# Block-diagonal global values, PSUM banks by token block and turned gate products in a local/global attention with top-k routing

## The chip, the cores and the metric

The kernel runs on one core of one Trainium2 chip. The metric is the device time of one execution in microseconds (us); lower is better. Each kernel is timed in several runs and the median is given. A separate execution is recorded by the hardware profiler, and all durations below come from that one.

## The reference

The first half is attention over 8 batches, 8 heads, 512 local and 32 global tokens of 64 elements. Global queries see all 544 keys; a local query sees the 32 global keys and the local keys at a distance of at most 32:

```
s_g  = scale * q_g @ k_all^T                      # k_all = [k_g, k_l]
out_g = softmax(s_g) @ v_all
s_l  = [scale * q_l @ k_g^T,  where(|i-j| <= 32, scale * q_l @ k_l^T, -1e9)]
out_l = softmax(s_l) @ v_all                      # x = concat(out_g, out_l): 4352 rows of 512
```

The second half sends each row of x to one of 8 experts and keeps the 80 rows with the largest gate of each expert:

```
logits = x @ w_gate;  expert = argmax;  gate = softmax(logits)[expert]
out[kept rows of e] = gate * (relu(x @ w1[e]) @ w2[e]);  all other rows are 0
```

## The kernel before, in words

A **quarter** q (16 of them) is half of a batch: four heads, two pairs j = 0, 1. A quarter passes through these chunks:

- `load_qk`, `load_v`: DMAs, one to two quarters ahead. `vb` holds the values of 32 global and 512 local tokens in five blocks, with a column of ones after each 64 (the softmax sum falls out of the product). `spread_v` on POOL makes a copy shifted by 64 partitions for the odd blocks.
- `T_chunk`: eight fp16 transposes on PE of the queries and keys of a pair, then two copies on ACT (L227) from PSUM into `qkT`. Rows were loaded with i = 4 neighbouring tokens in a partition, so the copy also reorders: it reads PSUM in order and writes every fourth element.
- `S_chunk`: scores. `G_ps` (global keys by all local queries), `gq_ps` (global queries), and `l_ps`, one bank per head: 8 blocks of 64 queries by a window of 128 keys. Even blocks are one product of 128 weight columns (L258); odd blocks are two of 64, each half written to the partitions that put its keys in the order of the shifted values (L266). ACT takes the exponential of each; DVE (first head of a pair) or POOL (second head) multiplies by the band mask (L273).
- `G_chunk`: values of the global keys, 16 products with 32 rows each (a head's 32 global keys lie in partitions 32h to 32h+31) into four PSUM tiles `o_ps`, one for each head (L289).
- `H_chunk(q, h)`: for head h, eight products `eL` by `vb`, which add to the head's bank (L302); then DVE's reciprocal of the sums and the scaling into `xn`.
- `Q_chunk`: the global queries' output. `X_chunk`: `xn` transposed (fp32, L333), copied by DVE to `xT`.
- `L_chunk(b)`: gate logits, 16 products for the local tokens with 128x128 of `xT` as weights and the 8 gate columns moving (L351), four for the global ones (L354); then softmax, argmax and first tie on DVE. `K_chunk` after batches 3, 6 and 7 runs rounds of max and replace on DVE (L412, L414) to find the 80 largest per expert.

After attention: the last selection rounds, the loading of the five experts that did not fit before (their memory is that of the attention), gather, two layers per expert, scatter. Weights of three experts are loaded during batches 0 to 2.

The order of chunks is that of the main loop, but a scheduler interleaves the instructions of neighbouring chunks on each engine; each engine then runs its own list in order. Pools give the buffers: two PSUM banks for `T` (T_ps, x_ps, lg), two for `S` (scores), four for `O` (o_ps, og). An fp32 product appears in the trace as two instructions, each with its weight load.

Of the kernel before, what the change touches and what calls it, by code (L numbers as in the profile page):

```python
# [18 lines left out]
P = 128  # L19
# [7 lines left out]
def _np_consts(B, S, SG, cap):  # L27
    c = {}
    c["ident16"] = np.eye(P, dtype=np.float16)
    c["identf"] = np.eye(P, dtype=np.float32)  # L30
    p = np.arange(P)[:, None]
    i = np.arange(64)[None, :]
    band = np.zeros((P, 8, 64), dtype=np.float32)
    for t in range(8):
        w = p if t % 2 == 0 else (p + 64) % P
        key = 64 * t + w
        band[:, t, :] = (w - i >= 0) & (w - i <= 2 * WIN) & (key >= SG) & (key < S)
    c["band"] = band
# [12 lines left out]
    rm5 = np.ones((P, NB, 8), dtype=np.float32)  # L51
    rm5[:, :, 0] = 0.0
    c["rmask5"] = rm5
    return c


@with_exitstack
def kernel(
# [37 lines left out]
    def psT(shape, dt, name):  # L96
        return ps.tile(shape, dt, tag="T", bufs=2, name=name)
# [4 lines left out]
    def psO(shape, dt, name):  # L102
        return ps.tile(shape, dt, tag="O", bufs=4, name=name)
# [45 lines left out]
    def load_v(b):  # L149
        v = vb[b % 2]  # L150
        nc.sync.dma_start(out=v[0:32, 0, :, 0:64], in_=v_g[b].rearrange("h g d -> g h d"))
        nc.sync.dma_start(out=v[32:128, 0, :, 0:64], in_=v_l[b, :, 0:96].rearrange("h g d -> g h d"))
        for u in range(1, 4):
            nc.sync.dma_start(out=v[:, u, :, 0:64],
                              in_=v_l[b, :, 128 * u - 32:128 * u + 96].rearrange("h p d -> p h d"))
        nc.sync.dma_start(out=v[0:32, 4, :, 0:64], in_=v_l[b, :, 480:512].rearrange("h g d -> g h d"))

    def spread_v(b):
        v = vb[b % 2]
        nc.gpsimd.tensor_copy(out=v[0:64, 5:9], in_=v[0:64, 1:5])  # L160
        nc.gpsimd.tensor_copy(out=v[64:128, 5:9], in_=v[64:128, 0:4])

    load_v(0)

    vgb = apool.tile([P, B, 2, 65], FP32, name="vgb")
    nc.vector.memset(vgb[:, :, :, 64:65], 1.0)
    nc.sync.dma_start(out=vgb[:, :, :, 0:64].rearrange("p b q d -> p (b q) d"),
                      in_=v_g.rearrange("b (q f) g d -> (f g) (b q) d", f=4))
    wg = cpool.tile([P, 4, E], FP32, name="wg")
    nc.sync.dma_start(out=wg, in_=moe_w_gate.rearrange("(c p) e -> p c e", p=P))  # L170

    wgq = cpool.tile([P, 4, E], FP32, name="wgq")
    for q in range(2):
# [38 lines left out]
    def T_chunk(q, j):  # L212
        b, qd = divmod(q, 2)
        pr = 2 * qd + j
        buf = qkT[(2 * q + j) % 4]
        for f in range(2):
            nc.gpsimd.tensor_copy(out=buf[64 * f:64 * f + 64, 512:544],  # L217
                                  in_=kbd[64 * f:64 * f + 64, b, pr, 32 * f:32 * f + 32])
        T_ps = psT([P, 2, 512], FP16, f"T_ps{q}_{j}")
        for t in range(2):  # L220
            for i in range(4):
                nc.tensor.transpose(out=T_ps[:, t, 128 * i:128 * i + 128],  # L222
                                    in_=qkr[q][:, t, i, 2 * j:2 * j + 2, :],
                                    identity=ident16[:, :])
        dst = buf[:, 0:1088].rearrange("x (t y) -> x t y", t=2)[:, :, 0:512]
        for t, eng in ((0, nc.scalar.copy), (1, nc.scalar.copy)):
            eng(out=dst[:, t].rearrange("x (p i) -> x i p", i=4),  # L227
                in_=T_ps[:, t].rearrange("x (i p) -> x i p", i=4))

    def S_chunk(q, j):  # L230
        b, qd = divmod(q, 2)
# [20 lines left out]
        s["eQ"].append(eQ)  # L252

        l_ps = [psS([P, 512], FP32, f"l_ps{q}_{j}_{hh}") for hh in range(2)]
        for t in range(0, 8, 2):
            for hh in range(2):
                o = 64 * hh
                nc.tensor.matmul(out=l_ps[hh][:, 64 * t:64 * t + 64],  # L258
                                 lhsT=buf[o:o + 64, 512 + 64 * t:640 + 64 * t],
                                 rhs=buf[o:o + 64, 64 * t:64 * t + 64], start=True, stop=True)  # L260
        for t in range(1, 8, 2):
            for half in range(2):
                for hh in range(2):
                    o = 64 * hh
                    k0 = 512 + 64 * (t + 1 - half)
                    nc.tensor.matmul(out=l_ps[hh][64 * half:64 * half + 64, 64 * t:64 * t + 64],  # L266
                                     lhsT=buf[o:o + 64, k0:k0 + 64],
                                     rhs=buf[o:o + 64, 64 * t:64 * t + 64], start=True, stop=True)
# [7 lines left out]
    def G_chunk(q):  # L276
        b, qd = divmod(q, 2)
        s = st[q]
        bs = bst.setdefault(b, {})
        if qd == 0:  # L280
            bs["xg"] = lpool.tile([P, 2, 64], FP32, tag="xgn", name=f"xgn{b}")
            bs["xb"] = lpool.tile([P, 4, XW], FP32, tag="xb", name=f"xb{b}")
            bs["xT"] = []
        s["o"] = [psO([P, 4, 65], FP32, f"o_ps{q}_{h}") for h in range(4)]
        s["xn"] = hpool.tile([P, 4, 256], FP32, tag="xn", name=f"xn{q}")
        for u in range(4):
            for h in range(4):
                r = slice(32 * h, 32 * h + 32)
                nc.tensor.matmul(out=s["o"][h][:, u, :], lhsT=s["eG"][r, 128 * u:128 * u + 128],  # L289
                                 rhs=vgb[r, b, qd, :], start=(u == 0), stop=False,  # L290
                                 skip_group_check=True)

    def H_chunk(q, h):
        b, qd = divmod(q, 2)
        s = st[q]
        v = vb[b % 2]
        hd = 4 * qd + h
        o = s["o"][h]
        for u in range(4):
            for odd in range(2):  # L300
                t = 2 * u + odd
                nc.tensor.matmul(out=o[64 * odd:64 * odd + 64, u, :], lhsT=s["eL"][h][:, 64 * t:64 * t + 64],  # L302
                                 rhs=v[:, 5 * odd + u, hd, :], start=False, stop=(u == 3),
                                 skip_group_check=True)
        rec = hpool.tile([P, 4], FP32, tag="rec", bufs=4)
        nc.vector.reciprocal(out=rec[:], in_=o[:, :, 64])  # L306
        nc.vector.tensor_tensor(out=s["xn"][:, :, 64 * h:64 * h + 64], in0=o[:, :, 0:64],  # L307
                                in1=rec[:].unsqueeze(2).to_broadcast([P, 4, 64]), op=ALU.mult)

    def Q_chunk(q):  # L310
# [16 lines left out]
    def X_chunk(q, j):  # L327
        b, qd = divmod(q, 2)
        s = st[q]
        bs = bst[b]  # L330
        x_ps = psT([P, 512], FP32, f"x_ps{q}_{j}")
        for u in range(4):
            nc.tensor.transpose(out=x_ps[:, 128 * u:128 * u + 128],  # L333
                                in_=s["xn"][:, u, 128 * j:128 * j + 128], identity=identf[:, :])
        xT = hpool.tile([P, 512], FP32, tag="xT", bufs=5, name=f"xT{q}_{j}")
        nc.vector.tensor_copy(out=xT[:], in_=x_ps[:])  # L336
        bs["xT"].append(xT)
        if j == 1:
            nc.gpsimd.tensor_copy(out=bs["xb"][:, :, 128 * qd:128 * qd + 128].bitcast(BF16), in_=s["xn"][:])

    def L_chunk(b):
# [118 lines left out]
    for q in range(NQ):  # L460
# [28 lines left out]
                K_chunk(g)  # L489
            pending = None  # L490
        H_chunk(q, 2)
        X_chunk(q, 0)
        if nxt:
            S_chunk(q + 1, 1)
        H_chunk(q, 3)
        Q_chunk(q)
        X_chunk(q, 1)
        st.pop(q)
        if qd == 1:
# [148 lines left out]
```

## Time and profile before

| | us |
|---|---|
| median of 3 runs (lowest to highest) | 457.93 (449.67 to 462.68) |
| the profiled execution's own time | 452.65 |
| its span, first to last instruction | 450.9 |
| PE busy | 332.3 (74%) |
| DVE, POOL, ACT busy | 212.5, 173.8, 142.5 |

The span has a long first part with attention, in which PE is busy nearly all of the time (from 18 to 340 us), and a second part of about 110 us with little work on PE until the last 38 us. [...] The record of the clock begins at 47 us; what the views show as 1.0 before that is not a record.

### The profile page before, as it was taken

How to read it: one execution, taken by the hardware profiler on the slowest of the kernel's cores; microseconds unless marked ns; L12 is line 12 of the kernel's file. 1: busy time of each engine (PE TensorE's matmuls, PEld its weight loads, DVE VectorE, ACT ScalarE, POOL GpSimd, SP SyncE). 2: the span in 40 equal slices, each digit the busy share in tenths (PEclk: the TensorE clock that was granted, in tenths of full speed). 3: DMA queues.
4: the chain of work that ended last, by engine and by line, in shares of the span. 5: the costliest groups of instructions: out<-in, count | busy, mean ns of one | idle time of the engine just before them, and what ended most of it. 6: DMA issues, size and time to landing. Idle time of an engine off the chain costs nothing. (4 is left out here: it accounts for less than half of the span.)

```text
span 450.9 us, 10118 instructions
## 1 busy us (share of the span) xinstructions
PE 332.3 (74%) x4268; PEld 271.3 (60%) x4268; DVE 212.5 (47%) x558; ACT 142.5 (32%) x201; POOL 173.8 (39%) x248
## 2 busy tenths in 40 slices
PE   0289899989999998989998999889961001203984
PEld 0268678878777887868886878778861000202662
DVE  4262633452733544298257633534755998200221
ACT  1193362374266256243524233563000000000221
POOL 6273660763755534255341532132140143311131
PEclk9999956598579569578658555895565555555999
DMA  9999799799999468215005400101011099998111
GB/s 151 174 197 341 121 173 190 254 138 192 185 201 173 91 197 135 34 51 100 6 12 94 92 4 1 48 6 34 17 27 49 4 199 208 210 210 161 31 45 44
DMA packets 84525, 51.87 MB, mean 115 GB/s; under 512 B 48472, under 2 KB 77568, under 8 KB 84480
## 3 DMA queue, kind: packets, MB, share of 16 engines
q0 software_dynamic: 34896, 27.75, 39.8%
q1 hardware_dynamic: 49584, 23.48, 20.6%
q8 instruction: 33, 0.54, 0.5%
q14 instruction: 12, 0.10, 0.1%
HBM read 62.25 MB, written 14.70 MB: 171 GB/s over the span
## 5 line engine op out<-in xcount | busy, mean ns | idle before, releaser
L227 ACT COPY qkT<-T_ps 128x512 f16<-128x512 f16 x64 | 77.7, 1369 | 94.0 <-PE T_ps L222 94.0
L273 POOL TENSOR_TENSOR eL<-eL,band 128x512 f32<-128x512 f32 x32 | 42.3, 1321 | 80.6 <-ACT eL L271 70.2
L302 PE MATMUL o_ps<-vb,eL 128*64 128x65 f32 x1024 | 70.2, 281 | 0.1
L302 PEld LDWEIGHTS o_ps<-vb,eL 128*64 128x64 f32 x1024 | 55.3, 184 | 9.4 <-issue 3.1
L271 ACT ACTIVATE eL<-l_ps 128x512 f32<-128x512 f32 x64 | 37.0, 600 | 60.6 <-PE l_ps L266 59.0
L289 PE MATMUL o_ps<-vgb,eG 32*128 32x65 f32 x512 | 52.6, 363 | 0.9 <-DVE xgn L324 0.7
L351 PE MATMUL lg<-wg,xT 128*128 128x8 f32 x256 | 46.2, 318 | 5.8 <-ACT qkT L227 5.3
L289 PEld LDWEIGHTS o_ps<-vgb,eG 32*128 32x128 f32 x512 | 45.8, 263 | 7.5 <-issue 4.8
L351 PEld LDWEIGHTS lg<-wg,xT 128*128 128x128 f32 x256 | 44.7, 271 | 7.5 <-ACT qkT L227 6.0
L273 DVE TENSOR_TENSOR eL<-eL,band 128x512 f32<-128x512 f32 x32 | 26.1, 819 | 28.6 <-ACT eL L271 28.6
L217 POOL COPY qkT<-kbd 64x32 f16<-64x32 f16 x64 | 16.1, 251 | 55.4 <-PE l_ps L258 43.3
L602 ACT ACTIVATE hT<-h_ps 128x320 bf16<-128x320 f32 x16 | 7.0, 437 | 94.8 <-PE h_ps L600 94.2
L306 DVE RECIPROCAL rec<-o_ps 128x4 f32<-128x4 f32 x64 | 10.6, 171 | 43.4 <-PE o_ps L302 42.9
L333 PE MATMUL x_ps<-identf,xn 128*128 128x128 f32 x128 | 28.6, 366 | 2.9 <-DVE xn L307 2.2
L222 PE MATMUL T_ps<-ident,qkr 128*128 128x128 f16 x256 | 26.5, 261 | 1.4 <-DVE kbd L198 0.9
L130 DVE COPY qkr<-qk 128x1024 f16<-128x1024 f16 x32 | 21.3, 686 | 12.9 <-DMA qk<-in_q_l_dram 6.7
L336 DVE COPY xT<-x_ps 128x512 f32<-128x512 f32 x32 | 21.8, 680 | 11.1 <-PE x_ps L333 10.8
L307 DVE TENSOR_TENSOR xn<-o_ps,rec 128x256 f32<-128x256 f32 x64 | 26.3, 416 | 1.2
L258 PE MATMUL l_ps<-qkT 64*128 64x64 f16 x256 | 22.6, 221 | 3.9 <-ACT eQ L251 3.7
L317 PE MATMUL og<-vb,eQ 128*32 128x65 f32 x640 | 25.3, 279 | 0.0
L358 DVE COPY L<-lg 128x32 f32<-128x32 f32 x8 | 1.5, 191 | 50.4 <-PE lg L354 50.4
L535 PE MATMUL thr_ps<-dthr,ones 8*128 8x8 f32 x2 | 0.6, 351 | 33.6 <-DVE dthr L533 33.6
(109 smaller groups left out, 501.1 us busy)
## 6 DMA issues: line engine op xcount, KB each, us to landing
out_dram<-zt SPq DMA_DIRECT2D x17, 512.0 KB, 6.2
w1sb<-in_moe_w_dram POOLq DMA_DIRECT2D x8, 1024.0 KB, 13.6
w2sb<-in_moe_w_dram POOLq DMA_DIRECT2D x8, 1024.0 KB, 17.4
vb<-in_v_l_dram SPq DMA_DIRECT2D x24, 256.0 KB, 6.4
x_scr<-xb SPq DMA_DIRECT2D x8, 514.0 KB, 3.3
qk<-in_q_l_dram POOLq DMA_DIRECT2D x16, 256.0 KB, 4.8
qk<-in_k_l_dram POOLq DMA_DIRECT2D x16, 256.0 KB, 5.1
vb<-in_v_l_dram SPq DMA_DIRECT2D x8, 192.0 KB, 7.2
```

What stands on the lines that cost most here:

```text
L222: nc.tensor.transpose(out=T_ps[:, t, 128 * i:128 * i + 128], in_=qkr[q][:, t, i, 2 * j:2 * j + 2, :], identity=ident16[:, :])
L227: eng(out=dst[:, t].rearrange("x (p i) -> x i p", i=4), in_=T_ps[:, t].rearrange("x (i p) -> x i p", i=4))
L258: nc.tensor.matmul(out=l_ps[hh][:, 64 * t:64 * t + 64], lhsT=buf[o:o + 64, 512 + 64 * t:640 + 64 * t], rhs=buf[o:o + 64, 64 * t:64 * t + 6 ...
L271: nc.scalar.activation(out=eL[:], in_=l_ps[hh][:], func=AF.Exp, scale=scale)
L273: eng.tensor_tensor(out=eL[:], in0=eL[:], in1=band[:].rearrange("p t i -> p (t i)"), op=ALU.mult)
L289: nc.tensor.matmul(out=s["o"][h][:, u, :], lhsT=s["eG"][r, 128 * u:128 * u + 128], rhs=vgb[r, b, qd, :], start=(u == 0), stop=False, skip_ ...
L302: nc.tensor.matmul(out=o[64 * odd:64 * odd + 64, u, :], lhsT=s["eL"][h][:, 64 * t:64 * t + 64], rhs=v[:, 5 * odd + u, hd, :], start=False, ...
L307: nc.vector.tensor_tensor(out=s["xn"][:, :, 64 * h:64 * h + 64], in0=o[:, :, 0:64], in1=rec[:].unsqueeze(2).to_broadcast([P, 4, 64]), op=A ...
L317: nc.tensor.matmul(out=og[32 * h:32 * h + 32, :], lhsT=s["eQ"][h // 2][:, u, 32 * (h % 2):32 * (h % 2) + 32], rhs=v[:, u, 4 * qd + h, :], ...
L333: nc.tensor.transpose(out=x_ps[:, 128 * u:128 * u + 128], in_=s["xn"][:, u, 128 * j:128 * j + 128], identity=identf[:, :])
L336: nc.vector.tensor_copy(out=xT[:], in_=x_ps[:])
L351: nc.tensor.matmul(out=lg[:, u, :], lhsT=bs["xT"][cc][:, 128 * u:128 * u + 128], rhs=wg[:, cc, :], start=(cc == 0), stop=(cc == 3))
```

## The change

- `vbd` (two buffers, loaded per batch by four DMAs) holds the global values of a quarter block-diagonally: rows 32f to 32f+31 carry head f's values in columns 65f to 65f+64 and zeros elsewhere. One product with 128 rows and 260 columns replaces four with 32 rows and 65 columns each, per block u of 128 queries.
- `H_chunk(q, u)` now does one block of 128 tokens for all four heads, into one bank per block; `G_chunk` has no products of its own.
- The odd key windows are written by DVE into `kO` with their 64-key halves swapped, so that an odd block is also one product of 128 weight columns.
- The two copies of `T_chunk` stay on ACT, but write in order and read PSUM in steps of 128 elements; keys come first.
- `X_chunk`'s copy moves from DVE to ACT; both X chunks come after `Q_chunk`; `xT` has 4 buffers for 5.
- Gate logits: four products with the gate weights (8 columns padded to 32) as weights and 512 tokens of `xT` moving, each into its own 32 partitions of one bank; ACT copies the bank; four products with a selection matrix `sel` sum the four parts and turn them.

```diff
+    sel = np.zeros((P, 8), dtype=np.float32)          # sel[32*cc : 32*cc+8] = eye(8)
...
+        for f in range(4):
+            nc.sync.dma_start(out=vbd[b % 2][32 * f:32 * f + 32, :, f, 0:64],
+                              in_=v_g[b].rearrange("(q f) g d -> f g q d", f=4)[f])
...
-        for t, eng in ((0, nc.scalar.copy), (1, nc.scalar.copy)):
-            eng(out=dst[:, t].rearrange("x (p i) -> x i p", i=4),
-                in_=T_ps[:, t].rearrange("x (i p) -> x i p", i=4))
+        nc.scalar.copy(out=dst[:, 1].rearrange("x (p i) -> x p i", i=4),
+                       in_=T_ps[:, 1].rearrange("x (i p) -> x p i", i=4))
+        halves = buf[:, 512:1152].rearrange("x (u y) -> x u y", y=64)
+        for w in range(2):
+            nc.vector.tensor_copy(out=kO[(2 * q + j) % 4][:, :, w, :], in_=halves[:, 2 - w:10 - w:2, :])
+        nc.scalar.copy(out=dst[:, 0]...)               # the queries, in the same way
...
+        for t in range(8):                             # S_chunk
             for hh in range(2):
+                lhsT = buf[o:o + 64, 512 + 64 * t:640 + 64 * t]   # even t; odd t: kO[o:o + 64, t // 2]
+                nc.tensor.matmul(out=l_ps[hh][:, 64 * t:64 * t + 64], lhsT=lhsT,
                                  rhs=buf[o:o + 64, 64 * t:64 * t + 64], start=True, stop=True)
...
-                nc.tensor.matmul(out=s["o"][h][:, u, :], lhsT=s["eG"][r, 128 * u:128 * u + 128],
-                                 rhs=vgb[r, b, qd, :], start=(u == 0), stop=False,
+    def H_chunk(q, u):
+        o = psO([P, 4, 65], FP32, f"o_ps{q}_{u}")
+        nc.tensor.matmul(out=o[:].rearrange("p h d -> p (h d)"), lhsT=s["eG"][:, 128 * u:128 * u + 128],
+                         rhs=vbd[b % 2][:, qd].rearrange("p h d -> p (h d)"), start=True, stop=False,
+        for h in range(4):
             for odd in range(2):
                 t = 2 * u + odd
+                nc.tensor.matmul(out=o[64 * odd:64 * odd + 64, h, :],
+                                 lhsT=s["eL"][h][:, 64 * t:64 * t + 64],
+                                 rhs=v[:, 5 * odd + u, 4 * qd + h, :], start=False, stop=True,
...
-        nc.vector.tensor_copy(out=xT[:], in_=x_ps[:])
+        nc.scalar.copy(out=xT[:], in_=x_ps[:])
...
+        for cc in range(4):                            # L_chunk
+            nc.tensor.matmul(out=lt_ps[32 * cc:32 * cc + 32, :], lhsT=wg[:, cc, :], rhs=bs["xT"][cc][:],
+        nc.scalar.copy(out=lt[:], in_=lt_ps[:])
         for u in range(4):
-            for cc in range(4):
-                nc.tensor.matmul(out=lg[:, u, :], lhsT=bs["xT"][cc][:, 128 * u:128 * u + 128],
-                                 rhs=wg[:, cc, :], start=(cc == 0), stop=(cc == 3))
+            nc.tensor.matmul(out=lg[:, u, :], lhsT=lt[:, 128 * u:128 * u + 128], rhs=sel[:],
```

Three places show how the lists move. On PE, at the seam of two quarters in batch 2 (og is `Q_chunk`'s output, the last number of a name is a buffer), before, from the global values to the second head:

```order
L289 MATMUL o_ps_3_1288<-vgb,eG_1113 128x65
L302 MATMUL o_ps_0_1285<-vb_88,eL_0_0_1149 64x65 x8
L222 MATMUL T_ps_1_1319<-ident_76,qkr_1267 128x128
L302 MATMUL o_ps_1_1286<-vb_88,eL_0_1_1152 64x65 x8
L241 MATMUL G_ps_1341<-qkT_120,kbd 64x512
```

and at a seam of the changed kernel, from the last scores of a quarter to its first block of values:

```order
L279 MATMUL l_ps_1_1_2032<-qkT_135,kO_139 128x64
L309 MATMUL o_ps_3_2055<-vb_89,eL_1_1_1850 64x65
L325 MATMUL og_2068<-vb_89,eQ_0_1726 32x65 x2
L341 MATMUL x_ps_0_2092<-identf,xn_1929 128x128 x4
L341 MATMUL x_ps_1_2099<-identf,xn_1929 128x128 x4
L303 MATMUL o_ps_0_2141<-vbd_96,eG_1974 128x260
L233 MATMUL T_ps_0_2125<-ident_76,qkr_2120 128x128
L309 MATMUL o_ps_0_2141<-vb_88,eL_0_0_2002 64x65 x2
L309 MATMUL o_ps_0_2141<-vb_88,eL_1_1_2052 64x65 x2
```

(Rows of the same chunk between these are left out.) The first block of values needed `eL` of one head before, and needs that of all four heads now, eL_1_1 of the scores just above among them.

The gate logits of a batch on PE, before:

```order
L344 MATMUL xgT_ps_1384<-identf,xgn_764 128x128
L302 MATMUL o_ps_2_1287<-vb_88,eL_1_0_1209 64x65
L351 MATMUL lg_1388<-wg,xT_0_941 128x8
L351 MATMUL lg_1388<-wg,xT_1_1025 128x8
L351 MATMUL lg_1388<-wg,xT_0_1171 128x8
L351 MATMUL lg_1388<-wg,xT_1_1255 128x8
```

(these four come three times in a row, then the scores of one head, then once more) and now:

```order
L358 MATMUL lt_ps_2221<-xT_0_1895,wg 32x512
L279 MATMUL l_ps_0_0_2193<-qkT_136 128x64
L358 MATMUL lt_ps_2221<-xT_1_1902,wg 32x512
L358 MATMUL lt_ps_2221<-xT_0_2097,wg 32x512
L358 MATMUL lt_ps_2221<-xT_1_2104,wg 32x512
L303 MATMUL o_ps_2_2316<-vbd_96,eG_1974 128x260
L364 MATMUL lg_2228<-sel,lt 128x8 x4
L367 MATMUL lg_2228<-wgq,xgT 32x8 x4
```

One wide product stands ahead of a head's scores, three follow together, and the sums come some 20 products later.

ACT's list around the seam, before:

```order
L271 ACTIVATE eL_1_0_2574<-l_ps_1_0_2548 128x512
L271 ACTIVATE eL_1_1_2577<-l_ps_1_1_2549 128x512
L227 COPY qkT_118<-T_ps_0_2634 128x4x128 x2
L227 COPY qkT_119<-T_ps_1_2679 128x4x128 x2
L251 ACTIVATE eQ_0_2712<-gq_ps_0_2706 128x320
```

and now:

```order
L283 ACTIVATE eL_1_0_2049<-l_ps_1_0_2031 128x512
L283 ACTIVATE eL_1_1_2052<-l_ps_1_1_2032 128x512
L344 COPY xT_0_2097<-x_ps_0_2092 128x512
L344 COPY xT_1_2104<-x_ps_1_2099 128x512
L237 COPY qkT_136<-T_ps_0_2125 128x512
L243 COPY qkT_136<-T_ps_0_2125 128x512
L237 COPY qkT_137<-T_ps_1_2156 128x512
L267 ACTIVATE eQ_0_2191<-gq_ps_0_2185 128x320
```

The two `xT` copies stand between the exponentials and the copies of the transposes.

## Rows read from the trace of the kernel before

**Rows 1.** The page: span, and the granted clock in 40 slices

```profile
span 450.9 us, 10118 instructions
PEclk9999956598579569578658555895565555555999
```

**Rows 2.** Timeline (start, length, engine, line, work), the tail, POOL and PE

```profile
358.45 0.76 POOL L439 DMA_DIRECT2D w1sb<-in_moe_w_dram  x1 [16.16 <-DVE merged L433]
413.41 0.76 PE L590 MATMUL xT_ps<-identbf,xg 80*128 80x80 bf16 x8 [27.03 <-DMA xg<-x_scr,idx]
```

**Rows 3.** Windows: busy time of PE, PEld, DVE, ACT, POOL; clock; DMA share; GB/s

```profile
47.00:340.00 293.00, 271.70 (x3545) 227.33 (x3543) 145.66 (x418) 117.81 (x161) 124.57 (x185) 0.69 0.51 98
91.40:108.50 17.10, 14.75 (x268) 12.22 (x267) 7.96 (x21) 11.18 (x15) 10.44 (x19) 1.00 1.07 167
108.50:129.00 20.50, 19.88 (x235) 16.43 (x234) 9.82 (x26) 6.64 (x10) 11.86 (x16) 0.50 1.04 212
```

**Rows 4.** L351, gate logits: its busy tenths in the same 40 slices

```profile
busy tenths in 40 slices 0000009009009204900970009049092000000000
```

**Rows 5.** Timeline of PE, half clock, end of one quarter to the next

```profile
112.26 1.14 PE L302 MATMUL o_ps<-vb,eL 128*64 128x65 f32 x16
...
116.42 0.39 PE L258 MATMUL l_ps<-qkT 64*128 64x64 f16 x4
...
117.77 1.30 PE L317 MATMUL og<-vb,eQ 128*32 128x65 f32 x38
...
119.20 1.06 PE L333 MATMUL x_ps<-identf,xn 128*128 128x128 f32 x4
...
124.13 1.99 PE L289 MATMUL o_ps<-vgb,eG 32*128 32x65 f32 x24
...
128.08 1.07 PE L302 MATMUL o_ps<-vb,eL 128*64 128x65 f32 x16
```

**Rows 6.** Timeline of PE, full clock, the next quarter

```profile
129.55 0.68 PE L302 MATMUL o_ps<-vb,eL 128*64 128x65 f32 x14
131.02 0.27 PE L258 MATMUL l_ps<-qkT 64*128 64x64 f16 x4 [0.78 <-ACT eQ L251]
...
135.28 0.65 PE L317 MATMUL og<-vb,eQ 128*32 128x65 f32 x30
135.87 0.66 PE L333 MATMUL x_ps<-identf,xn 128*128 128x128 f32 x4
136.36 0.61 PE L222 MATMUL T_ps<-ident,qkr 128*128 128x128 f16 x8
136.90 1.90 PE L289 MATMUL o_ps<-vgb,eG 32*128 32x65 f32 x32
138.73 0.69 PE L302 MATMUL o_ps<-vb,eL 128*64 128x65 f32 x16
...
139.90 0.69 PE L302 MATMUL o_ps<-vb,eL 128*64 128x65 f32 x16
```

**Rows 7.** Timeline of PE: gate logits of batches 1 and 7

```profile
106.14 3.18 PE L351 MATMUL lg<-wg,xT 128*128 128x8 f32 x24 [1.12 <-ACT qkT L227]
...
332.07 7.00 PE L351 MATMUL lg<-wg,xT 128*128 128x8 f32 x32 [0.52 <-DVE xT L336]
339.00 0.60 PE L354 MATMUL lg<-wgq,xgT 128*32 128x8 f32 x8
```

**Rows 8.** Groups of the page: copies, exponentials, mask, logits (busy, mean ns | idle before)

```profile
L227 ACT COPY qkT<-T_ps 128x512 f16<-128x512 f16 x64 | 77.7, 1369 | 94.0 <-PE T_ps L222 94.0
L273 POOL TENSOR_TENSOR eL<-eL,band 128x512 f32<-128x512 f32 x32 | 42.3, 1321 | 80.6 <-ACT eL L271 70.2
L271 ACT ACTIVATE eL<-l_ps 128x512 f32<-128x512 f32 x64 | 37.0, 600 | 60.6 <-PE l_ps L266 59.0
L351 PE MATMUL lg<-wg,xT 128*128 128x8 f32 x256 | 46.2, 318 | 5.8 <-ACT qkT L227 5.3
L336 DVE COPY xT<-x_ps 128x512 f32<-128x512 f32 x32 | 21.8, 680 | 11.1 <-PE x_ps L333 10.8
```

More of the change, by code (lines that the diff above doesn't have):

```diff
@@ L53, in _np_consts @@
     c["rmask5"] = rm5
+    sel = np.zeros((P, 8), dtype=np.float32)
+    for cc in range(4):
+        sel[32 * cc:32 * cc + 8] = np.eye(8, dtype=np.float32)
+    c["sel"] = sel
     return c
@@ L161, in spread_v @@
         nc.gpsimd.tensor_copy(out=v[64:128, 5:9], in_=v[64:128, 0:4])
-    load_v(0)
[L165 to L170, printed above, removed]
+    vbd = [apool.tile([P, 2, 4, 65], FP32, name=f"vbd{i}") for i in range(2)]
+    for i in range(2):
+        nc.gpsimd.memset(vbd[i][:], 0.0)
+        for f in range(4):
+            nc.gpsimd.memset(vbd[i][32 * f:32 * f + 32, :, f, 64:65], 1.0)
+    load_v(0)
+    wg = cpool.tile([P, 4, 32], FP32, name="wg")
+    nc.gpsimd.memset(wg, 0.0)
+    sel = const("sel", FP32)
+    nc.sync.dma_start(out=wg[:, :, 0:E], in_=moe_w_gate.rearrange("(c p) e -> p c e", p=P))
     wgq = cpool.tile([P, 4, E], FP32, name="wgq")
@@ L202 @@
     qkT = [apool.tile([P, 1152], FP16, name=f"qkT{i}") for i in range(4)]
+    kO = [apool.tile([P, 4, 2, 64], FP16, name=f"kO{i}") for i in range(4)]
     for i in range(4):
@@ L225, in T_chunk @@
         dst = buf[:, 0:1088].rearrange("x (t y) -> x t y", t=2)[:, :, 0:512]
-        for t, eng in ((0, nc.scalar.copy), (1, nc.scalar.copy)):
-            eng(out=dst[:, t].rearrange("x (p i) -> x i p", i=4),
-                in_=T_ps[:, t].rearrange("x (i p) -> x i p", i=4))
+        nc.scalar.copy(out=dst[:, 1].rearrange("x (p i) -> x p i", i=4),
[3 more added lines that the diff above has]
+            nc.vector.tensor_copy(out=kO[(2 * q + j) % 4][:, :, w, :], in_=halves[:, 2 - w:10 - w:2, :])
+        nc.scalar.copy(out=dst[:, 0].rearrange("x (p i) -> x p i", i=4),
+                       in_=T_ps[:, 0].rearrange("x (i p) -> x p i", i=4))
     def S_chunk(q, j):
@@ L254, in S_chunk @@
         l_ps = [psS([P, 512], FP32, f"l_ps{q}_{j}_{hh}") for hh in range(2)]
-        for t in range(0, 8, 2):
+        ko = kO[(2 * q + j) % 4]
+        for t in range(8):
             for hh in range(2):
                 o = 64 * hh
-                nc.tensor.matmul(out=l_ps[hh][:, 64 * t:64 * t + 64],
-                                 lhsT=buf[o:o + 64, 512 + 64 * t:640 + 64 * t],
-                                 rhs=buf[o:o + 64, 64 * t:64 * t + 64], start=True, stop=True)
[L261 to L268, printed above, removed]
+                if t % 2 == 0:
+                    lhsT = buf[o:o + 64, 512 + 64 * t:640 + 64 * t]
+                else:
+                    lhsT = ko[o:o + 64, t // 2].rearrange("x w y -> x (w y)")
+                nc.tensor.matmul(out=l_ps[hh][:, 64 * t:64 * t + 64], lhsT=lhsT,
+                                 rhs=buf[o:o + 64, 64 * t:64 * t + 64], start=True, stop=True)
         for hh in range(2):
@@ L296, in H_chunk @@
         v = vb[b % 2]
-        hd = 4 * qd + h
-        o = s["o"][h]
-        for u in range(4):
+        o = psO([P, 4, 65], FP32, f"o_ps{q}_{u}")
+        nc.tensor.matmul(out=o[:].rearrange("p h d -> p (h d)"), lhsT=s["eG"][:, 128 * u:128 * u + 128],
+                         rhs=vbd[b % 2][:, qd].rearrange("p h d -> p (h d)"), start=True, stop=False,
+                         skip_group_check=True)
+        for h in range(4):
             for odd in range(2):
                 t = 2 * u + odd
-                nc.tensor.matmul(out=o[64 * odd:64 * odd + 64, u, :], lhsT=s["eL"][h][:, 64 * t:64 * t + 64],
-                                 rhs=v[:, 5 * odd + u, hd, :], start=False, stop=(u == 3),
+                nc.tensor.matmul(out=o[64 * odd:64 * odd + 64, h, :],
+                                 lhsT=s["eL"][h][:, 64 * t:64 * t + 64],
+                                 rhs=v[:, 5 * odd + u, 4 * qd + h, :], start=False, stop=True,
                                  skip_group_check=True)
@@ L306, in H_chunk @@
         nc.vector.reciprocal(out=rec[:], in_=o[:, :, 64])
-        nc.vector.tensor_tensor(out=s["xn"][:, :, 64 * h:64 * h + 64], in0=o[:, :, 0:64],
+        nc.vector.tensor_tensor(out=s["xn"][:, u].rearrange("p (h d) -> p h d", h=4), in0=o[:, :, 0:64],
                                 in1=rec[:].unsqueeze(2).to_broadcast([P, 4, 64]), op=ALU.mult)
@@ L347, in L_chunk @@
         nc.vector.tensor_copy(out=xgT[:], in_=xgT_ps[:])
+        lt_ps = psT([P, 512], FP32, f"lt_ps{b}")
+        for cc in range(4):
+            nc.tensor.matmul(out=lt_ps[32 * cc:32 * cc + 32, :], lhsT=wg[:, cc, :], rhs=bs["xT"][cc][:],
+                             start=True, stop=True, skip_group_check=True)
+        lt = lpool.tile([P, 512], FP32, tag="lt", bufs=1)
+        nc.scalar.copy(out=lt[:], in_=lt_ps[:])
         lg = psT([P, NB, E], FP32, f"lg{b}")
         for u in range(4):
-            for cc in range(4):
-                nc.tensor.matmul(out=lg[:, u, :], lhsT=bs["xT"][cc][:, 128 * u:128 * u + 128],
-                                 rhs=wg[:, cc, :], start=(cc == 0), stop=(cc == 3))
+            nc.tensor.matmul(out=lg[:, u, :], lhsT=lt[:, 128 * u:128 * u + 128], rhs=sel[:],
+                             start=True, stop=True)
         for h4 in range(4):
@@ L491 @@
         H_chunk(q, 2)
-        X_chunk(q, 0)
         if nxt:
@@ L496 @@
         Q_chunk(q)
+        X_chunk(q, 0)
         X_chunk(q, 1)
```

8 lines of the change are left out of this document (1 added, 7 removed).

## The prediction

> **What bounds the kernel now.** I began with the page's slices [rows 1]: from the second slice to about the 30th PE is the work, and its granted clock jumps between the two levels 0.5 and 1.0. The timeline of the end [rows 2] closes off the other part: the last gate logits end at 339.60 [rows 7], then come selection rounds on DVE, the loading of the late experts, for which POOL waits 16.16 us on DVE, and expert layers, for which PE waits 27.03 us on DMA. From 339.60 to the span's end at 450.9 are 111.3 us; the change touches nothing there. What it can win must come from the attention.
>
> There the windows [rows 3] show PE busy 271.70 of 293.00 us, and no other engine above half, so PE sets the pace. Its mean clock is 0.69: 0.19 / 0.5 = 38% of the time at full clock (111 us), 182 us at half. Such a row is "busy" time, not work: the stretch from 108.50 to 129.00 has PE busy 97% at clock 0.50, the one before it 86% at 1.00. The timelines of PE price the clock. A quarter at half clock, from one group of value products to the same place a quarter later, runs from 112.26 to 128.08, 15.8 us [rows 5]; at full clock from 129.55 to 139.90, 10.35 us [rows 6], with a wait of 0.78 us on ACT in it. **One quarter costs 5.5 us more at half clock**, and a batch's 32 logit products 7.0 us at half clock [rows 7], against some 4 at full (the 24 from 106.14, where the clock falls on the way, took 3.18).
>
> Where does the clock fall? Laying the logits' busy slices [rows 4] under the clock's digits [rows 1], it drops to 5 in slices 5, 7, 10, 13, 16, 20, 22 and 27 (counted from 0), and six of these eight (all but 5 and 22) have logits in the same slice or the one before. The products there move only 8 columns over a fresh 128x128 weight block.
>
> **The change, part by part,** first at an unchanged clock pattern. Nine quarters or so ran at half clock (182 us over 15.8 plus half a batch's logits, 3.5), about seven at full.
> 1. *Odd key blocks as one product.* Eight of 24 score products of a pair go. Four products took 0.39 us at half clock and 0.27 at full. If time goes by columns the pair's 24 (about 1.35, the 64-column halves lying side by side in part, to 0.90) save up to a third; if by instruction less. I take 0.30 per pair at half, 0.17 at full: -0.6 and -0.34 per quarter; bounds 0 and -0.9.
> 2. *Block-diagonal values.* 32 instructions with 32 rows and 65 columns become 8 with 128 rows and 260 columns: the same 2,080 columns. The old 24 took 1.99 us at half clock, so 32 take 2.65, and at full 1.90 [rows 5, 6]. Were the old ones side by side by row groups, the new cost up to 4.0 at half; if not, 2.6. I take 3.6 and 1.9, near the upper end at half: +1.0 and 0 per quarter.
> 3. Terms 1 and 2: 9 x 0.4 - 7 x 0.34 = +1 us. They nearly cancel; PE's count of instructions falls, not its columns.
> 4. *Logits.* 32 instructions become 8 of 512 columns, 8 small sums. The four parts write four groups of 32 partitions, as og's 38 products of 65 columns did, which took 1.30 us in all [rows 5], 34 ns each, where a value product takes 1.14 / 16 = 71 ns: they ran side by side. The first stands apart and three together, so I take two rounds, each of two passes of 512 columns; x_ps moves 512 columns in 1.06 us at half clock [rows 5] and 0.66 at full [rows 6]. That is some 4 us at half clock and 2 at full, and with 1.7 and 1.0 for the eight sums 5.7 against 7.0, or 3.0 against 4: -1.1 per batch, **-9 us** in all. One after the other the eight take 8 and 4: 9.7 against 7.0, or 5 against 4, +15 in all.
> 5. *ACT.* The copies of the transposes took 1369 ns each, where the exponential of as many elements took 600 [rows 8]; the copy writes every fourth 2-byte element. Written in order they cost between 0.60 and 1.37; I take 0.65, the nearest row being the same engine's read of as many elements. Four per quarter save 2.9; two xT copies add 1.2 there, and leave DVE, 680 each [rows 8]. kO's two copies per pair go to DVE in their place, and DVE has room [rows 3]. PE's logits waited 5.3 us in all for these copies [rows 8], the exponential eQ behind them held PE by 0.78 in the full-clock quarter [rows 6]; 5.3 + some four of these: **-8 us**, bounds -10 and 0.
> 6. The block-diagonal values' loads (four DMAs per batch on SP) and the smaller xT pool cost nothing while they arrive a batch early; cover gone would show as PE waiting at the first block of a batch, one DMA share of 1.04 to 1.07 there already [rows 3].
>
> Sum: +1 - 9 - 8 = -16 us. The profiled execution's own time is 452.65, 5.3 under the median of 457.93 (runs from 449.67 to 462.68), so at the old clock pattern it comes to 437.
>
> **The clock.** The logits in six of the eight falls are replaced by wide products, and PE loses the waits on ACT. If those falls go, 6/8 of nine half-clock quarters, 6.75, gain 5.5 plus about half of a batch's 3 us: 7 each, **-47 us**. Against it I hold back 8: batches 0 to 2 move expert weights at a DMA share of 1.04 to 1.07 whatever the clock, and a faster PE meets the new wait on all four heads (below). So 437 - 47 + 8 = **398 us**.
>
> What speaks against it in rows: a busy share of 97% did not lift the clock from 0.50 between 108.50 and 129.00, so PE's being busy is not what it follows. [...]
>
> **Rivals.**
> - **Forecast, 50%** (375 to 420; another 5% lies below): most falls vanish.
> - **Clock as before, 24%: about 437** (425 to 445). The falls in slices 5 and 22 have no logits near, so the clock can fall for other reasons; the sums still move 8 columns, and the gate product's weights fill 32 columns only. If PE merely runs shorter, the sum above is all.
> - **ACT gives nothing, 13%: 440 to 467.** The new copy reads PSUM in steps of 128 elements. If that is as slow as the old write, 5.5 us of copies per quarter stay, the xT copies' 1.2 come on top, in front of the transposes' copies, and PE's waits grow by up to that: 437 + 8 = 445, and with 16 x 1.2 = 19 up to 464. The row of 1369 against 600 ns shows only that the old access is slow. [...]
> - **The first block's wait, 8%: slower, 468 to 490.** Before, a head's values waited for that head alone; now the first block waits for all four. Behind the last scores stand two exponentials (0.60 each) and POOL's mask (1.32): 2.5 us. The cover on PE is og (0.65), x_ps (0.66), the wide product (about 0.5) and transposes (0.61) at full clock [rows 6], 2.4 us, so little is left open if ACT and POOL are ready. If ACT's copies or POOL's other work delay the chain so that all 2.5 us show, 16 quarters lose 40: 437 + 40 = 477, with the clock falling in each gap. It decides slower from (467 - 437) / 16 = 1.9 us per quarter. POOL's 124.57 busy of 293.00 us [rows 3] speaks against.
>
> **Range and chances.** About 2% is what a measurement of this kernel tells from no change: 448.8 to 467.1. Range 372 to 442: the forecast, most of the second case, and the low end of the third; serial logits inside the forecast (2 us more per batch at full clock) give 414. Faster by over 2%: the first case with its lower tail (55%), nearly all of the second (23%) and a little of the third (2%), 80%. Within 2%: 12%, mostly the third. Slower: 8%. The forecast's own range is 375 to 420.
>
> **What would show it.** The clock's digits from the fifth to the 29th slice mostly at 9, and none falling where logits stand: the forecast; the old pattern: the second case. ACT's transposes' copies at about 0.65 us mean confirm term 5, at 1.3 the third case. The 260-column products' spacing checks term 2, and the span of a batch's eight wide products term 4: 4 us at half clock or 2 at full if side by side, twice that if not. PE's idle time in front of the value products, put down to eL by POOL or ACT, is the fourth case. The late weights' load should start near 305 instead of 358.45. It is wrong if the end part moves by more than a few us or if DMA becomes what PE waits for in the first batches.

## The result

The changed kernel takes **371.88 us** (median of 4 runs, 370.75 to 375.93), against 453.80 for the kernel before (4 runs, 447.41 to 462.68). The ratio is 0.828, 95% interval 0.817 to 0.838: 17% faster. A second set of 6 runs on another occasion gave 373.89 (0.834, 0.828 to 0.841). The forecast was 398. The first median lies 0.12 us under the range of 372 to 442, the second inside it, and both are below the forecast case's own 375 to 420. Executions of one kernel differ by how long the attention ran at half clock (164 to 239 us in those of the kernel before); so the table of the experiments gives that for all runs.

The page of the changed kernel, its span and the granted clock of TensorE in 40 slices (PEclk, in tenths of full speed); and, from the view of the wide logit products (L358), their busy tenths in the same slices:

```profile
span 370.6 us, 8739 instructions
...
PEclk9996999879877899999998999998555555557999
```

```profile
busy tenths in 40 slices 0000006005000600600600060606000000000000
```

Against [rows 1] and [rows 4]: from the fifth to the 28th slice there are 7s, 8s and 9s, where 11 of the 26 digits from the fifth to the 30th were 5 before. Of the eight groups of logits two (slices 6 and 9, counted from 0) still have a dip in the next slice, and the last one (27) stands where the attention ends; the dips that are left (slices 7 and 8, 10 to 13, 21) are short.

Windows (busy time of PE, PEld, DVE, ACT, POOL; granted clock; DMA share; GB/s), from 18 us to the end of the last gate logits, before and in the changed kernel, and the end part of the latter:

```profile
18.00:339.60 321.60, 298.22 (x3871) 247.56 (x3871) 159.25 (x443) 134.03 (x183) 140.05 (x205) 0.72 0.57 112
```

```profile
18.00:259.10 241.10, 216.61 (x3103) 153.07 (x3103) 151.60 (x475) 115.93 (x223) 141.25 (x205) 0.93 0.76 149
...
258.00:370.00 112.00, 35.08 (x408) 24.53 (x408) 48.41 (x102) 7.23 (x17) 26.06 (x30) 0.64 0.62 117
```

The attention ends 80.5 us earlier, at 259.1; from there to the span's end are 111.5 us, where 111.3 stood: the whole gain is in the attention. PE's idle time there is 241.10 - 216.61 = 24.5 us, and was 23.4. So PE did not wait less in sum: its busy time shrank by 81.6 us. The mean clock went from 0.72 to 0.93, so the time at half clock from 2 x 0.28 x 321.6 = 180 us to 2 x 0.07 x 241.1 = 34. (Before, nothing ahead of 47 us is on record; in the changed kernel the 6 in slice 3 counts. The 146 us less are rather too few.) The late experts' load starts 80.7 us earlier than in [rows 2] (timeline, POOL):

```profile
277.71 0.75 POOL L452 DMA_DIRECT2D w1sb<-in_moe_w_dram  x1 [15.95 <-DVE merged L446]
```

The timeline of PE in the changed kernel, a batch's logits and one quarter at full clock (start, length; the products of L303 are the wide values, og the global queries):

```profile
118.28 1.08 PE L303 MATMUL o_ps<-vbd,eG 128*128 128x260 f32 x2
...
124.37 1.04 PE L358 MATMUL lt_ps<-xT,wg 128*32 128x512 f32 x2
...
125.68 1.06 PE L358 MATMUL lt_ps<-xT,wg 128*32 128x512 f32 x6
...
128.28 1.06 PE L364 MATMUL lg<-sel,lt 128*128 128x8 f32 x8
129.27 0.42 PE L367 MATMUL lg<-wgq,xgT 128*32 128x8 f32 x8
...
134.86 0.76 PE L325 MATMUL og<-vb,eQ 128*32 128x65 f32 x36
...
138.90 0.66 PE L303 MATMUL o_ps<-vbd,eG 128*128 128x260 f32 x2
...
145.20 0.77 PE L325 MATMUL og<-vb,eQ 128*32 128x65 f32 x40
```

From og at 134.86 to og at 145.20 is a quarter without logits (less four of its og products): 10.34 us without a wait. The 10.35 us of [rows 6] are not a whole quarter, as told below; the second head's products of one quarter and the next start at 128.08 and 139.90, with 11.04 us of busy time between them in the kernel before:

```profile
128.08:139.90 11.82, 11.04 (x222) 9.22 (x221) 5.67 (x16) 8.40 (x11) 7.02 (x13) 0.96 1.15 152
```

The first 0.92 us of that ran at half clock, so it is an estimated 10.7 us at full clock. **At full clock a quarter's work on PE costs nearly what it did.** Six wide logit products of three partition groups took 1.06 us, two of one group 1.04: the groups ran side by side, as assumed. The logits take 2.1 + 1.06 us where the old ones took 7.00 at half clock and, by the prediction's estimate from 3.18 us for 24 of the 32, some 4 at full [rows 7].

Groups of the page (busy, mean ns of one | idle before), to be read against [rows 8]:

```profile
L344 ACT COPY xT<-x_ps 128x512 f32<-128x512 f32 x32 | 17.7, 588 | 48.5 <-PE x_ps L341 48.4
...
L237 ACT COPY qkT<-T_ps 128x512 f16<-128x512 f16 x32 | 18.9, 590 | 31.2 <-PE T_ps L233 28.6
```

The copies that read PSUM in steps of 128 elements take 590 ns, where the stepped write took 1369, and as long as an unstepped copy of as many fp32 elements (588).

### The profile page after: what moved, and what is told of

It reads as the page before. It is cut to its first block, busy times and chain, and to the rows that moved or that the text cites. A ratio compares the mean times of both kernels' runs of the same rounds, so it can differ in the third digit from the quotient of the medians.

```text
span 370.6 us, 8739 instructions
## 1 busy us (share of the span) xinstructions
PE 250.6 (68%) x3500; PEld 176.6 (48%) x3500; DVE 205.5 (55%) x589; ACT 124.4 (34%) x241; POOL 177.3 (48%) x259
## 5 line engine op out<-in xcount | busy, mean ns | idle before, releaser
L309 PE MATMUL o_ps<-vb,eL 128*64 128x65 f32 x1024 | 62.9, 239 | 7.4 <-DVE eL L285 4.0
L309 PEld LDWEIGHTS o_ps<-vb,eL 128*64 128x64 f32 x1024 | 45.5, 142 | 26.9 <-issue 12.5
L303 PE MATMUL o_ps<-vbd,eG 128*128 128x260 f32 x128 | 47.1, 452 | 0.0
L283 ACT ACTIVATE eL<-l_ps 128x512 f32<-128x512 f32 x64 | 36.9, 596 | 24.7 <-PE l_ps L279 24.0
L134 DVE COPY qkr<-qk 128x1024 f16<-128x1024 f16 x32 | 23.4, 743 | 21.8 <-DMA qk<-in_q_l_dram 14.6
L344 ACT COPY xT<-x_ps 128x512 f32<-128x512 f32 x32 | 17.7, 588 | 48.5 <-PE x_ps L341 48.4
L237 ACT COPY qkT<-T_ps 128x512 f16<-128x512 f16 x32 | 18.9, 590 | 31.2 <-PE T_ps L233 28.6
L341 PE MATMUL x_ps<-identf,xn 128*128 128x128 f32 x128 | 23.0, 315 | 4.2 <-DVE xn L315 4.2
L303 PEld LDWEIGHTS o_ps<-vbd,eG 128*128 128x128 f32 x128 | 20.9, 206 | 8.4 <-issue 6.7
L279 PE MATMUL l_ps<-qkT,kO 64*128 64x64 f16 x256 | 21.5, 191 | 2.9 <-DVE kO L242 2.9
L242 DVE COPY kO<-qkT 128x256 f16<-128x256 f16 x64 | 19.1, 337 | 3.7 <-ACT qkT L237 3.6
L279 PEld LDWEIGHTS <-qkT 64*128 64x128 f16 x256 | 15.4, 95 | 11.6 <-issue 8.7
```

The source lines that it names most:

```text
L134: nc.vector.tensor_copy(out=qkr[q][:, t].rearrange("p i h d -> p h i d"), in_=qks[q][:, t])
L237: nc.scalar.copy(out=dst[:, 1].rearrange("x (p i) -> x p i", i=4), in_=T_ps[:, 1].rearrange("x (i p) -> x p i", i=4))
L242: nc.vector.tensor_copy(out=kO[(2 * q + j) % 4][:, :, w, :], in_=halves[:, 2 - w:10 - w:2, :])
L279: nc.tensor.matmul(out=l_ps[hh][:, 64 * t:64 * t + 64], lhsT=lhsT, rhs=buf[o:o + 64, 64 * t:64 * t + 64], start=True, stop=True)
L303: nc.tensor.matmul(out=o[:].rearrange("p h d -> p (h d)"), lhsT=s["eG"][:, 128 * u:128 * u + 128], rhs=vbd[b % 2][:, qd].rearrange("p h d ...
L309: nc.tensor.matmul(out=o[64 * odd:64 * odd + 64, h, :], lhsT=s["eL"][h][:, 64 * t:64 * t + 64], rhs=v[:, 5 * odd + u, 4 * qd + h, :], star ...
```

## The experiments

Each row is one edit. "End" is when the last gate logits end in the profile; "half" is the time at half clock ahead of that. The latter is 2 x (1 - mean clock) x span, less the 80.5 us at half clock that the end part has in the changed kernel, over all runs of a kernel; the ratio is to the kernel before in runs taken with it. The record of the clock begins at 47 us in the profile of the kernel before and at 24 in that of the changed one, and what lies ahead of it counts as full clock, so differences of less than some 20 us in the last column say nothing.

| kernel | median us | ratio to before (95%) | end, us | half, us |
|---|---|---|---|---|
| before | 453.80 to 462.05 | 1 | 339.6 | 180 (profile), 164 to 239 |
| changed, two sets | 371.88, 373.89 | 0.828 (0.817 to 0.838), 0.834 (0.828 to 0.841) | 259.1, 260.0 | 19 to 44 |
| before + new logits | 414.46 | 0.924 (0.901 to 0.948) | 302.7 | 102 to 119 |
| before + new copies | 437.08 | 0.969 (0.945 to 0.994) | 323.4 | 159 to 221 |
| before + both | 400.68 | none given | 291.0 | 86 to 120 |
| changed, old logits | 394.52 | 0.879 (0.870 to 0.888) | 281.5 | 95 to 116 |
| changed, stepped write | 403.21 | 0.892 (0.882 to 0.902) | 292.5 | 44 to 58 |
| changed, head banks | 389.40 | 0.841 (0.830 to 0.852) | 280.1 | 81 to 116 |
| the same, full rows | 385.12 | 0.851 (0.841 to 0.860) | 273.9 | 27 to 68 |
| changed, odd halves | 378.87 | 0.822 (0.810 to 0.834) | 266.6 | 20 to 34 |
| changed, xT on DVE | 380.18 | 0.833 (0.825 to 0.841) | 270.5 | 28 to 45 |
| changed, weights later | 383.18 | 0.855 (0.851 to 0.860) | 268.8 | 40 to 44 |
| the same, rounds spread | 382.90 | 0.855 (0.845 to 0.864) | 268.5 | 30 to 45 |

**Old logits in the changed kernel.**

```diff
-        for cc in range(4): nc.tensor.matmul(out=lt_ps[...], lhsT=wg[:, cc, :], rhs=bs["xT"][cc][:], ...)
-            nc.tensor.matmul(out=lg[:, u, :], lhsT=lt[:, 128 * u:128 * u + 128], rhs=sel[:], ...)
+            for cc in range(4):
+                nc.tensor.matmul(out=lg[:, u, :], lhsT=bs["xT"][cc][:, 128 * u:128 * u + 128],
+                                 rhs=wg[:, cc, 0:E], start=(cc == 0), stop=(cc == 3))
```

> The changed kernel with the gate logits as before: 32 instructions a batch with the xT blocks as weights and 8 columns moving. Theory L (the logits' 8-column products are what makes the clock fall): falls come back in or right behind the logits' slices, six or more of them, and a quarter at half clock follows each; 372 + 7 x 7 + 8 x 1 = about 425 (405 to 440), clock in the attention near 0.75. Theory W (PE's waits on the slow copies made it fall) and theory V (the 32-row value products did): only the products' own difference, some 1 us a batch, about 380 (374 to 388), clock near 0.93.

Its clock, and the logits' busy tenths:

```profile
PEclk9995698697599589579958979958655555556998
```

```profile
busy tenths in 40 slices 0000009009009007900900390900900000000000
```

A fall stands at every group of logits again, which is theory L; W and V alone cannot give 394.5. But the time at half clock is 95 to 116 us, where the kernel before has 164 to 239, so the price was 22 us and not 50, and theory L's range was missed too. Something else in the change lets the clock rise sooner.

**New logits in the kernel before** (the same edit the other way, with the padded gate weights, `sel` and ACT's copy).

> The kernel before with only the gate logits turned (gate weights stationary, 512 tokens moving, ACT's copy of 0.6 us, the sums by sel). Theory L: six of the eight falls go, 454 - 9 - 40 = about 405 (390 to 420). Theories W and V: the clock's digits stay as they were, only the products' own 1 to 2 us a batch are saved: about 443 (435 to 452).

```profile
PEclk9999997589967978988966557799655555555999
```

414 lies in theory L's range. Half-clock time goes by 60 to 80 us, not by the 135 that six falls of eight were to be worth: 6s and 5s stay in slices 20 to 23, without the old logits.

**Stepped write in the changed kernel.**

```diff
-        nc.scalar.copy(out=dst[:, 1].rearrange("x (p i) -> x p i", i=4), in_=T_ps[:, 1].rearrange("x (i p) -> x p i", i=4))
+        nc.scalar.copy(out=dst[:, 1].rearrange("x (p i) -> x i p", i=4), in_=T_ps[:, 1].rearrange("x (i p) -> x i p", i=4))
...                                                    # and so for the queries, dst[:, 0]
```

> The changed kernel with the two copies of the transposes reading PSUM in order and writing every fourth element, as before (keys still first). All theories: these copies take about 1.37 us instead of 0.59. Theory L: PE waits some more on ACT, eight or so of 1 to 2 us, 372 + 12 = about 384 (376 to 395), clock still above 0.88 in the attention. Theory W: the waits bring the falls back, above 410 with the clock below 0.8.

Waits of PE in this kernel (engine, tile, line, what it waited for: us in total, times, longest):

```profile
PE G_ps L257 <- ACT qkT L243: 12.8, 17, 1.4
PE lt_ps L358 <- ACT qkT L243: 9.0, 7, 1.5
...
PE l_ps L279 <- ACT eQ L267: 4.7, 4, 1.3
```

Neither theory had the size: 403. The changed kernel has none of these three waits, 26.5 us in all. Other waits are shorter here, so of the 33.4 us by which the attention ends later 15.3 are more idle time of PE (39.8 for 24.5) and 18.1 more busy time. The clock stays high (mean 0.89), as theory L said, though 44 to 58 us at half clock for 19 to 44 leave room for a small part of theory W.

**New copies in the kernel before** (that edit the other way).

> The kernel before with only the copies' access turned (write in order, read PSUM in steps of 128 elements). Copies 0.59 us instead of 1.37 in all theories. Theory L: PE's waits on ACT go, 454 - 8 = about 446 (440 to 452), the falls stay with the logits. Theory W: most falls go, 400 to 420. Theory V: as L.

437, a little under theory L's range; the clock's falls stay (mean 0.69 in the profiled execution's attention). In the profiles the copies alone move the end by 16.2 us, 8.8 of them less idle time of PE (14.6 for 23.4), with hardly less time at half clock; the interval of the ratio is wide. Against theory W this is the clearest run.

**Both in the kernel before.**

> The kernel before with both the turned gate logits and the copies that write in order; values, odd key blocks, xT's engine and the order of the chunks stay. Alone the logits left the attention's end at 302.7 and the copies at 323.4, from 339.6. If these two are all that matters and independent, 339.6 - 37 - 16 = 287, a time of about 400 (392 to 406). If shorter waits also keep the clock up once the logits are gone, as in the changed kernel (theory W as an addition to L): 372 to 385. If the rest of the change (block-diagonal values, odd blocks) is what lifts the clock the rest of the way (theory V): 395 to 410 with 80 us or more at half clock in the attention.

400.7. The two add up (36.9 + 16.2 = 53.1 us expected at the end, 48.6 found in a profile of 400.88 us; the quickest run took 391.62), and shorter waits do not bring the clock up: 86 to 120 us at half clock are left. So some 20 to 30 of the 80.5 us are in the rest of the change.

**Head banks in the changed kernel.**

```diff
-        o = psO([P, 4, 65], FP32, f"o_ps{q}_{u}")      # H_chunk(q, u), with the product of 260 columns
+        s["o"] = [psO([P, 4, 65], FP32, f"o_ps{q}_{h}") for h in range(4)]
+        for u in range(4):                              # G_chunk; H_chunk(q, h) as before
+            for h in range(4):
+                r = slice(32 * h, 32 * h + 32)
+                nc.tensor.matmul(out=s["o"][h][:, u, :], lhsT=s["eG"][r, 128 * u:128 * u + 128],
+                                 rhs=vbd[b % 2][r, qd, h, :], start=(u == 0), stop=False, ...)
```

> The changed kernel with the values by head as before: 16 products of 32 rows and 65 columns into four banks, one per head, and then each head's eight products. Theory V (work in the 128-row product holds the clock up): half-clock time in the attention rises from 34 us to 70 or more, 390 to 405. Without V only the products' cost counts: four wide products took 2.3 us at full clock against 1.83 for the old sixteen, and the first group no longer waits for all four heads: 372 - 8 = about 364 (358 to 374).

Its clock, and the window of its attention:

```profile
PEclk9996999599569869979855585986555555556999
```

```profile
18.00:280.10 262.10, 241.78 (x3487) 187.25 (x3487) 156.54 (x476) 114.88 (x223) 140.12 (x205) 0.79 0.69 137
```

389, with 81 to 116 us at half clock: theory V, which the prediction did not have. That is what the kernel before with both edits has left (86 to 120), so the odd blocks, `xT`'s engine and the order of the chunks are not needed to explain the clock. All four runs (383 to 394 us) are above the ten of the changed kernel (371 to 376), although the old products are the cheaper ones at full clock; as the intervals of the ratios touch, the loss of time is less sure than that of the clock. This edit also changes banks and waits, so the next run keeps those.

**The same with full rows.**

```diff
-                nc.tensor.matmul(out=s["o"][h][:, u, :], lhsT=s["eG"][r, 128 * u:128 * u + 128],
-                                 rhs=vbd[b % 2][r, qd, h, :], ...)
+                nc.tensor.matmul(out=s["o"][h][:, u, :], lhsT=s["eG"][:, 128 * u:128 * u + 128],
+                                 rhs=vbd[b % 2][:, qd, h, :], ...)
```

> As the run with head banks (values by head into four banks), but each of the 16 products per quarter takes all 128 rows: the head's zero-extended block of vbd moves (65 columns), so rows of the other heads meet zeros. Same output, same banks, same waits, same columns as the wide product. If the work in the array is what holds the clock up, half-clock time falls from 112 us in the attention to below 65 and the time to 372 to 382, though these products cost up to 0.5 us a quarter more than the 32-row ones. If the banks by head and their waits brought the falls, half-clock time stays at 95 or more, 389 to 398.

```profile
PEclk9998999589996899959977999999555555556999
```

```profile
18.00:273.90 255.90, 243.45 (x3487) 200.44 (x3487) 157.35 (x476) 115.02 (x223) 140.56 (x205) 0.90 0.73 141
```

Same banks, same number of products, same columns, four times the rows, most of them against zeros: half-clock time falls to 27 to 68 us (mean clock 0.90 for 0.79). **So it is the products of 32 rows, not the banks by head, behind which the clock stays low here.** What the pair does not part is the rows and the longer time for which full rows keep PE busy: 75.6 us in all, where the 32-row products took 48.6 and the wide ones 47.1. For that reason the time, 385, is over the 372 to 382 expected and hardly below 389: at full clock 24 instructions took 0.90 us with 32 rows and 2.84 with 128 (timelines of PE, head banks and full rows), where the expectation had up to 0.5 us more for a quarter's 32.

```profile
119.57 0.90 PE L301 MATMUL o_ps<-vbd,eG 32*128 32x65 f32 x24
```

```profile
87.52 2.84 PE L300 MATMUL o_ps<-vbd,eG 128*128 128x65 f32 x24
```

**Odd halves; xT on DVE.**

```diff
-        nc.vector.tensor_copy(out=kO[...][:, :, w, :], in_=halves[:, 2 - w:10 - w:2, :])   # odd halves
+                    nc.tensor.matmul(out=l_ps[hh][64 * half:64 * half + 64, ...], lhsT=buf[o:o + 64, k0:k0 + 64], ...)
...
-        nc.scalar.copy(out=xT[:], in_=x_ps[:])          # xT on DVE, a kernel of its own
+        nc.vector.tensor_copy(out=xT[:], in_=x_ps[:])
```

> The changed kernel with each odd key block as two products of 64 columns again, and without kO and DVE's two copies for it. Product cost: 16 quarters by 0.2 to 0.4 us more on PE, DVE 19 us less: 374 to 380 if PE sets the pace, 366 to 372 if DVE's work in the way of eL costs more than the products save. Theory V in its other form (fewer columns fall the clock): above 385 with 60 us or more at half clock.

> The changed kernel with xT copied by DVE again. DVE gets 32 copies of 0.68 us, ACT loses 32 of 0.59. PE waits for DVE (xn, eL of the first heads, kO) more often than for ACT in the changed kernel, so slower: 376 to 384. If ACT's queue is what the transposes' copies wait in: 364 to 371.

Medians of 378.87 and 380.18, but ratios of 0.822 and 0.833 whose intervals overlap with the changed kernel's: whether either part is worth anything stays open, between nothing and 8 us. Neither moves the clock (20 to 34 and 28 to 45 us at half), so neither is a cause of the clock's rise.

**Weights later; rounds spread.** Two tries at something faster.

```diff
-        if qd == 1 and b < NRES: load_w(b, wpool)
+        if qd == 1 and b % 2 == 1 and b // 2 < NRES: load_w(b // 2, wpool)
...
+        run_rounds(3 if q < 14 else 4)                  # second kernel: after H_chunk 0, 1, 2 and the X chunks
```

> The changed kernel with the three resident experts' weights loaded in batches 1, 3 and 5 instead of 0, 1 and 2. In the changed kernel DVE's regrouping waits 14.6 us for the queries' and keys' loads in the first batches, where the DMA share is 0.9 and more, and three of the falls that are left lie there. If the loads are the next bound: 363 to 368. If not, or if the weights then stand in the way of later loads: 369 to 375.

> As the run with the weights later, and the selection rounds of batches 0 to 3 and 4 to 6 handed to DVE three (in the last two quarters four) at a time between the chunks of the next quarters, instead of all at one place. If DVE's rounds in the way of xn, kO and eL cost PE the 4 to 6 us that the two quarters with rounds are longer: 6 to 10 us below the run with the weights later, 355 to 361. If other work fills these waits, no difference; if the last rounds now end behind the last logits, up to 5 us slower.

> The changed kernel again, to be compared with the three others on the same chip: 370 to 376.

Both slower, by 9 us, on the chip where the changed kernel gave 373.89. Timeline of the first, POOL and PE:

```profile
81.38 1.91 POOL L168 COPY vb<-vb 64x2080 f32<-64x2080 f32 x1 [12.49 <-DMA x_scr<-xgb]
83.33 0.10 POOL L391 MEMSET oh<- 32x8 f32 x1
```

```profile
83.85 0.40 PE L412 MATMUL t_ps<-identf,sc_all 128*40 128x128 f32 x1 [11.18 <-DVE sc_all L397]
```

With the load in another place the scheduler put the next batch's value copy ahead of a small clearing on POOL; the copy waited 12.49 us for a DMA, DVE for the clearing, and PE 11.18 us for DVE (11.9 in the second kernel). That one wait covers the whole loss, and hid what the two edits were to show; they settle nothing on DMA or on the rounds. By its median no version tried beats the changed kernel.

## Why the prediction was right, and where not

**What bounds the kernel: right.** PE in the attention, with the end untouched (111.3 and 111.5 us).

**The price of half clock: read too low.** The stretches of [rows 5] and [rows 6] are not a whole quarter: both run from the third head's products to the second head's of the next quarter, three of its four heads and one of its two `G_ps` products. And they do not hold the same work: the one at half clock lacks 12 of the 48 score products. PE's busy time in them:

```profile
112.26:128.08 15.82, 15.20 (x187) 11.98 (x185) 9.06 (x24) 5.28 (x8) 11.83 (x16) 0.50 0.96 218
129.55:139.90 10.35, 9.57 (x202) 8.05 (x199) 4.60 (x13) 7.10 (x11) 6.99 (x12) 1.00 1.12 150
```

Twelve scores took 0.67 us at half clock (109.26 to 109.93), so 15.87 us of work at half clock stand against 9.57 at full: an estimated 40% of half-clock time is lost, and not 5.5 of 15.8 (35%).

**Clock: near the right size, by luck, and the wrong share.** At 40% the 146 us less at half clock are worth an estimated 58 us; -47 was taken. But the step that gave 6/8 of the half-clock quarters to the logits' falls failed. The logits alone took half-clock time from 180 to 108 us by profile (2 x 0.19 x 284.7; 102 to 119 over the runs), worth 29 us. The other 29 came with the wide value products: with head banks half-clock time is at 110 us again (2 x 0.21 x 262.1). The prediction priced those by columns alone, at +1 us with term 1, and did not ask what they do to the clock. That a share too large for the logits nearly made up for one left out is luck.

**Term 4, logits: -9, measured about -8** (36.9 us at the end in the kernel before, less the 29 of the clock). Side by side was right.

**Term 5, ACT: mis-sized.** -8 was taken, -10 the bound; alone the copies give -16.2 at the end of the attention in the profile. 0.65 us was right for the copy (0.59). The sum counted PE's waits at the logits and at the scores behind eQ, and left out two places in the kernel before:

```profile
PE gq_ps L248 <- ACT qkT L227: 2.9, 4, 0.9
PE G_ps L241 <- ACT qkT L227: 2.7, 7, 1.2
```

Taken out of the changed kernel the same edit costs 26.5 us of waits in front of G_ps, lt_ps and l_ps, and 33.4 at the end, twice the 16.2 that it is worth in the kernel before, where the mean clock is 0.72 and not 0.93.

**Terms 1 to 3: open in detail, small in sum.** 58 + 8 + 16 = 82 for 80.5 us; the parts are estimates that overlap, so the sum is no proof. Term 2 was too low: two instructions of the wide product took 0.60 to 0.71 us at full clock (from 136.49 to 142.51), some 2.7 a quarter, where 1.9 was taken. Head banks cost 21.0 us at the end, of which the clock's 76 us are 30, so the wide products themselves are an estimated 9 us dearer.

**Give-back: +8 taken, nothing found** in sum. By these estimates the clock (11), the copies (8) and the give-back (8) make up the 26 us between 398 and 372. What came late next are short waits of PE on DVE and POOL, in the changed kernel:

```profile
PE t_ps L412 <- DVE sc_all L397: 6.3, 3, 3.0
PE x_ps L341 <- DVE xn L315: 4.2, 4, 2.2
PE o_ps L309 <- DVE eL L285: 4.0, 3, 1.9
...
PE o_ps L309 <- POOL eL L285: 2.5, 4, 1.3
```

**The rivals.** The clock as before (437) is refuted. The stepped read of PSUM is not slow (590 ns, where the write in steps of 8 bytes took 1369), so the third case is too. PE's waits for eL in front of all value products came to 4.0 + 2.5 us, where 40 were needed for the fourth case; POOL and ACT were ready in time. That the clock falls in each gap of PE, as that case had it, no run shows: with the stepped write PE was idle for 39.8 us, at a mean clock of 0.89. PE was busy 92.7% of the time at a mean clock of 0.69 before [rows 3], and 89.8% at 0.93 in the changed kernel, so the clock does not follow the share of busy time here. That it follows the work in the array is the author's conjecture: the pair of head-bank runs fits it (81 to 116 us at half clock with 32 rows, 27 to 68 with 128), without proving it.

## What to carry to other kernels

Where PE is the bound, read the granted clock before counting products: here an estimated 50 to 60 of 80 us gained came from the clock, at a nearly unchanged cost of a quarter at full clock (10.34 us for an estimated 10.7). Price narrow products by what follows them too. The products of 8 columns over a 128x128 weight block came with half-clock time worth an estimated 29 us, beside an estimated 8 us of their own. Those of 32 rows came with half-clock time worth an estimated 30 us; the wide ones, padded with zeros, cost an estimated 9 us more themselves and were yet the faster choice (371 to 376 us against 383 to 394). Price a slow copy that others wait behind at the pace that the change will bring, not at the old one: here 33.4 us at the end of the attention, against 16.2.

## What the runs showed of the hardware

- ACT, 512 two-byte elements per partition from PSUM: 1369 ns with a write of every fourth element, 590 with the read in steps of 128 elements and the write in order. ACT's busy time in the attention went from 115.93 to 156.26 us with the edit turned back in the changed kernel, and from 134.03 to 93.47 with it alone in the kernel before.
- Value products of 65 columns at full clock: 24 instructions with 32 rows, in four groups of rows, took 0.90 us with head banks, and 24 with 128 rows 2.84: the groups of rows ran side by side. The changed kernel, without them, is the faster one all the same (371 to 376 us against 383 to 394).
- Gate products into four groups of 32 columns: six instructions of 512 columns, into three of the groups, took 1.06 us at full clock, and two into one group 1.04.
